# Preparing the queries for dK in a fused attention backward: one copy per 16 units, a 64 KB transpose, and a fourfold repeat through DRAM into a ring of two

## The chip, the cores and the metric

The kernel runs on one core of one Trainium2 chip. A core has a matrix engine (PE, with its weight loads listed apart as PEld), a vector engine (DVE), a scalar engine (ACT), a general engine (POOL, GpSimd) and SP, which issues DMAs; 16 DMA engines move the data. On-chip memory has 128 partitions (SBUF); PE writes to PSUM, eight banks of 128 x 512 floats. The metric is device microseconds of one execution, the median of several runs; lower is better.

## What is computed

The program is the forward output and all gradients of two attention layers side by side, on a sequence of 2048 tokens with width 448 and 16 heads of 28. Layer A is linear attention, layer B is softmax attention with a single key head and value head shared by the 16 query heads. Nearly all of the time goes into layer B:

```python
def _B_ref(x, wq, wk, wv, wo):
    q = (x @ wq).reshape(B, S, H, Dh).transpose(0, 2, 1, 3)
    k = x @ wk
    v = x @ wv
    scores = jnp.einsum("bhqd,bkd->bhqk", q, k) * (Dh ** -0.5)
    p = softmax(scores, axis=-1)
    o = jnp.einsum("bhqk,bkd->bhqd", p, v)
    return o.transpose(0, 2, 1, 3).reshape(B, S, H * Dh) @ wo
out  = concatenate([A(x_A, ...), B(x_B, ...)], axis=-1)
grads = vjp(out)(grad_out)      # for all eight inputs
```

For the backward pass of B the kernel needs, for every head, P (the exponentials), dP = dO V', dS = P * (dP - D), and from dS both dQ = dS K and dK = dS' Q, summed over all heads.

## The kernel before

Layer A and the projections of B come first (up to about 207 us of the span). Then one loop does the softmax attention of B, forward and backward fused. It is written out by hand under a manual schedule: the order of the code is the order of each engine's queue.

The loop counts units u. Two heads and 256 queries make a block b; there are 64 blocks (8 chunks qc of 256 queries, in each 8 pairs of heads), and each block has 8 units of 256 keys, so 512 units, and 28 more for the pipeline to run out. Pairs of heads lie two and two in a group g of four heads, so a group and a chunk make 16 units. What one unit issues:

- PE: the scores S of unit u and the products dP of unit w = u - 16 (rows_SD, L683), the sums for O and dQ (o_dq, L894, on even u), dV (dv_mm, L901, from u = 8b + 20), and dK (dk_m, L865, on odd u from u = 8b + 27).
- ACT: two exponentials into eT (L955, L997), and cp, a copy of half of dP out of PSUM (L971).
- DVE: the first half of dsT = dP * eT (L967), and a 32 x 32 block transpose of dsT into dsx (L1041), which dk_m reads.
- POOL: the second half of dsT (L972), and once per 8 units the small products prod, don, R (L821, L830, L831) and Dq, don (L836, L837, in row_D).
- SP: every fourth unit a DMA transpose of eT into eN, 1 MB (L999), which dv_mm reads. After five of the blocks, two or four token tiles of finished output are transposed as well (oTq, L1048).
- Spread over the units, the output projection of finished rows; a finished tile of 112 KB is stored by a DMA that POOL issues (L749).

dK needs the queries as weights in the order of dsx: in each of the four blocks of 32 partitions the same 32 queries, with the two of each pair of neighbours in separate tiles (s = 0, 1). That is qX. Until now it was made per chunk and group: qc_copy (L854) copies the 256 queries of a chunk and repeats them fourfold along the free dimension, one parity s at a time, into the staging tile qst; qc_T (L859) has SP transpose qst (256 KB) into a quarter of qX[qc]. There are two qX tiles of 256 KB x 4, one in use and one being filled, in the pools cqXa and cqXb. For chunk 0 this is done before the loop, half of the copies on DVE and half on POOL; for the next seven chunks at units 29, 30, 37, 38, 45, 46, 53 and 54 of each 64, all on POOL (the lines with gq and iq, L973 to L979 and L1001).

At u = 8b + 27 (L986) the finished dQ of block b is written over its queries, so these must have been read before.

Queues matter here in two places. POOL's instructions run in order, and a DMA that POOL issues stands among them: a wait of such a DMA holds up the dsT products behind it. SP's DMAs are issued in order as well, and a transpose is issued for as long as SP takes to describe it.

Of the kernel before, what the change touches and what calls it, by code (L numbers as in the profile page):

```python
# [11 lines left out]
BF16 = mybir.dt.bfloat16  # L12
# [5 lines left out]
P = 128  # L18
# [7 lines left out]
def kernel(  # L26
# [21 lines left out]
    nc = tc.nc  # L48
# [13 lines left out]
    dpool = ctx.enter_context(tc.tile_pool(name="dscr", bufs=1, space=bass.MemoryType.DRAM))  # L62
# [585 lines left out]
    NU = NB * 8  # L648
    qT_B = [R1[:, g, :] for g in range(4)]
    vaug, kn, do_nat = vaug_, kn_, R2x[:, 0:NS, :]  # L650
    with ExitStack() as cs_:
        pe_ = cs_.enter_context(tc.tile_pool(name="ceT", bufs=1, side="right"))
        pn_ = cs_.enter_context(tc.tile_pool(name="ceN", bufs=1, side="right"))
        pd_ = cs_.enter_context(tc.tile_pool(name="cdsT", bufs=5, side="right"))
        pqa_ = cs_.enter_context(tc.tile_pool(name="cqXa", bufs=1, side="right"))
        px_ = cs_.enter_context(tc.tile_pool(name="cdsx", bufs=2, side="right"))
        pqb_ = cs_.enter_context(tc.tile_pool(name="cqXb", bufs=1, side="right"))
        pc_ = cs_.enter_context(tc.tile_pool(name="ccp", bufs=3, side="right"))
        pw_ = cs_.enter_context(tc.tile_pool(name="cwk", bufs=4, side="right"))
        pp_ = cs_.enter_context(tc.tile_pool(name="cout", bufs=2, side="right"))  # L660
# [4 lines left out]
        dsT, dsx, qX, don, doT, rl, prod = ({} for _ in range(7))  # L665
# [3 lines left out]
        def eT(u):  # L669
            return ETs[u // 4 % 5][:, u % 4, :, :]  # L670
# [4 lines left out]
        def mmt(out, lhsT, rhs, pos, start, stop):  # L675
            nc.tensor.matmul(out, lhsT=lhsT, rhs=rhs, start=start, stop=stop, tile_position=pos,  # L676
                             skip_group_check=True)

        def blk(b):
            qc, pair = divmod(b, 8)  # L680
            return qc, pair, pair // 2, pair % 2
# [24 lines left out]

        woTp, gbT = R4, R2.rearrange("p t (c k) -> p t c k", k=P)

        qst = pp_.tile([P, 8, 4, 32], BF16, name="qst", bufs=1)[:, :, :, :]
        identF = pp_.tile([P, P], F32, name="identF", bufs=1)  # L710
        make_identity(nc, identF[:])
        oTs = pp_.tile([P, 256], F32, name="oTs", bufs=1)
# [89 lines left out]
        def due(u, lag):  # L802
            b, r = divmod(u - lag, 8)
            return b if r == 0 and 0 <= b < NB else None
# [28 lines left out]
        def row_D(b):  # L833
            Dq = pw_.tile([P, 2, 2, 1], F32, name="Dq")
            nc.vector.tensor_reduce(out=Dq[:, :, :, 0], in_=prod[b][:], axis=AX.X, op=ALU.add)
            nc.gpsimd.tensor_tensor(out=Dq[:], in0=Dq[:], in1=rl[b][:], op=ALU.mult)  # L836
            nc.gpsimd.tensor_tensor(out=don[b][:, :, :, 0:1], in0=Dq[:], in1=rl[b][:], op=ALU.mult)  # L837
# [13 lines left out]
            doT[b] = pw_.tile([P, 256], BF16, name="doT", bufs=2)  # L851
            nc.vector.tensor_copy(out=doT[b][r:r + 64, :], in_=tps2.pop(b)[r:r + 64, 0:256])  # L852

        def qc_copy(eng, st, qc, g, s):  # L854
            src = qT_B[g][:, qc * 256:(qc + 1) * 256].rearrange("p (b j s) -> p b j s", b=4, s=2)[:, :, :, s]
            eng.tensor_copy(out=st.rearrange("p (b s) a j -> p b s a j", s=2)[:, :, s, :, :],  # L856
                            in_=src.unsqueeze(2).to_broadcast([P, 4, 4, 32]))

        def qc_T(st, qc, g):  # L859
            nc.sync.dma_start_transpose(qX[qc].rearrange("p b s c -> p (b s) c")[:, :, g * P:(g + 1) * P],  # L860
                                        st.rearrange("p n a j -> p (n a j)"))

        dk_two = SB[2]

        def dk_m(b, m, other=0):  # L865
            qc, pair, g, hp = blk(b)
            h, B, s = m // 8, (m // 2) % 4, m % 2
            for a in range(4):
                rhs = dsx[b][32 * a:32 * a + 32, :, h, :, :].rearrange(
                    "p u t (b i s) -> p u t b i s", b=4, s=2)[:, :, :, B, :, s]  # L870
                k = 32 * ((a + 2) % 4) if other else 32 * a
                mmt((dk_two if other else dk_acc)[k:k + 32, :],
                    qX[qc][32 * a:32 * a + 32, B, s, pair * 64 + 32 * h:pair * 64 + 32 * h + 32],
                    rhs, (32 * a, k), other == 2 or b == 0 and m == 0, other == 0 and b == NB - 1 and m == 15)

        def o_mm(v):
# [44 lines left out]
        do_slots.update({32 + 8 * n: (13 + n // 4, n % 4 * P, n % 4 * P + P) for n in range(12)})  # L921
        with tc.manual_schedule():
            nc.sync.dma_start(wo, wo_d[:, 0:D].rearrange("(g p) c -> p g c", p=P))
            qX[0] = pqa_.tile([P, 4, 2, 512], BF16, name="qX")
            for g in range(4):
                st = pd_.tile([P, 2, 512], BF16, name="dsT").rearrange("p a (n j) -> p a n j", j=32).rearrange(
                    "p a (n b) j -> p (a n) b j", b=4)
                qc_copy(nc.gpsimd, st, 0, g, 0)
                qc_copy(nc.vector, st, 0, g, 1)
                qc_T(st, 0, g)  # L930
            for u in range(NU + 28):
                w = u - 16
                hasS = u < NU
# [5 lines left out]
                if u % 2 == 0:  # L939
                    b, n = divmod(u - 20, 8)  # L940
# [22 lines left out]
                if hasD:  # L963
                    dst = pd_.tile([P, 2, 512], BF16, name="dsT")
                    dsT[w] = dst
                    ew = eT(w)
                    nc.vector.tensor_tensor(out=dst[:, 0, :], in0=dp[0][:, :], in1=ew[:, 0, :], op=ALU.mult)  # L967
                    if (b := due(u, 12)) is not None:
                        row_D(b)
                    cp = pc_.tile([P, 512], BF16, name="cp")  # L970
                    nc.scalar.activation(out=cp[:, :], in_=dp[1][:, :], func=ACT.Copy)  # L971
                    nc.gpsimd.tensor_tensor(out=dst[:, 1, :], in0=cp[:, :], in1=ew[:, 1, :], op=ALU.mult)  # L972
                gq, iq = divmod(u % 64 - 29, 8)  # L973
                qq = u // 64 + 1
                if 0 <= gq < 4 and u < 448:
                    if gq == 0 and iq == 0:
                        qX[qq] = (pqb_ if qq % 2 else pqa_).tile([P, 4, 2, 512], BF16, name="qX")
                    if iq < 2:
                        qc_copy(nc.gpsimd, qst, qq, gq, iq)  # L979
                if u == 7:  # L980
                    nc.vector.memset(oTs[64:128, :], 0.0)
                if (b := due(u, 9)) is not None:
# [1 line left out]
                if (b := due(u, 27)) is not None:  # L984
                    qc, pair, g, hp = blk(b)
# [10 lines left out]
                if hasS:  # L996
                    nc.scalar.activation(out=eT(u)[:, 1, :], in_=sp[1][:, :], func=ACT.Exp, scale=scale)  # L997
                    if u % 4 == 3:
                        nc.sync.dma_start_transpose(ENs[u // 4 % 6][:, :, :],  # L999
                                                    ETs[u // 4 % 5][:, :, :, :].rearrange("p a b c -> p (a b c)"))  # L1000
                    if 0 <= gq < 4 and iq == 1 and u < 448:  # L1001
                        qc_T(qst, qq, gq)

                if u % 2:
                    b, i = divmod(u - 27, 8)
                    if 0 <= b < NB:
                        for m in range(2 * i, 2 * i + 4):
                            dk_m(b, m, (1 + (u == 519 and m == 2 * i + 1)) * (m % 2) if 519 <= u < 537 else 0)
                else:
                    o_dq((u - 2, u - 1), (u - 20, u - 19))  # L1010
# [26 lines left out]
                if 0 <= y < NU:  # L1037
                    b, tp = divmod(y, 8)
                    if tp == 0:
                        dsx[b] = px_.tile([P, 8, 2, 2, 256], BF16, name="dsx")  # L1040
                    nc.vector.transpose(  # L1041
                        out=dsx[b][:, tp, :, :, :].rearrange("p h t c -> p (h t c)").bitcast(F32),
                        in_=dsT[y][:, :, :].rearrange("p h c -> p (h c)").bitcast(F32))
# [20 lines left out]
        for c in range(4):  # L1064
            t = dkvT[0:32, :].rearrange("p (t a i) -> p t a i", a=4, i=32)[:, :, c, :]
            src = dk_acc[32 * c:32 * c + 32, :].rearrange("p (t i) -> p t i", i=32)
# [93 lines left out]
```

## Time and profile before

| | us |
|---|---|
| median of three runs | 1041.17 |
| lowest and highest | 1037.56, 1046.53 |
| the profiled execution | 1044.09 |
| its span on the core | 1042.4 |

The loop's first exponential (L955) starts at 207.09 us, its last at 968.48 us; the tail (dK and dV out, dWq, dX) ends at 1042.4. The granted clock of PE is 1.0 throughout. In the rows of the profile the first number of a pair is busy time in us, the second the mean of one instruction in ns, and behind the bar stands the time that the engine was idle just before these instructions, with who ended it. Instructions of one engine can overlap at their ends: three ACT instructions of some 640 ns each start every 480 to 500 ns. Some other groups:

| line, engine, what | count | mean ns |
|---|---|---|
| L967 DVE, first half of dsT | 512 | 665 |
| L1041 DVE, block transpose into dsx | 512 | 697 |
| L955, L971, L997 ACT | 512 each | 636, 639, 651 |
| L427 POOL, a copy of 128 x 256 (layer A) | 4 | 399 |
| L749 POOL, issue of a store of 112 KB | 16 | 582 |
| L538 POOL, issue of a store of 224 KB | 8 | 724 |
| L94 POOL, issue of a load of 448 KB | 4 | 760 |
| L999 SP, issue of a transpose of 1 MB | 128 | 5440 (median) |
| L860 SP, issue of a transpose of 256 KB | 32 | 1264 (median) |

### The profile page before, as it was taken

To read this page: it belongs to the slowest core of one execution; us is meant where nothing else is said; L and a number is where in the kernel's file an instruction comes from. 1 tells how busy PE (TensorE), PEld (TensorE's weight loads), DVE (VectorE), ACT (ScalarE), POOL (GpSimd) and SP (SyncE) were. 2 spreads that over 40 slices of the span, in tenths; PEclk is the share of its full clock that TensorE was granted. 3 is DMA by queue.
4 is the path that set the end of the run, shared out by engine and by line. 5 is a ranking of instruction groups with operands and counts; after the bars stand their busy time and mean duration, and the time that the engine had idled before them with its cause. 6 is when DMAs were issued, how large, how long until landed. Compare 5 with 4: busy or idle time off the path is not lost.

```text
span 1042.4 us, 40109 instructions
## 1 busy us (share of the span) xinstructions
PE 1003.5 (96%) x16245; PEld 485.1 (47%) x16245; DVE 886.9 (85%) x1780; ACT 865.2 (83%) x1743; POOL 812.3 (78%) x1106
## 2 busy tenths in 40 slices
PE   9999999999999999999999999999999999999998
PEld 5555554434444444444444444444444444444444
DVE  7897500669999999999999999999999999999942
ACT  6463132599999999999999999999999999999632
POOL 8601282238998998999999989998999999889860
PEclk9999999999999999999999999999999999999999
DMA  9879999299999999999999999999999999999983
GB/s 261 157 137 191 176 229 218 38 161 201 194 187 192 187 193 194 202 187 194 201 193 195 192 187 204 198 182 202 188 197 186 195 195 195 200 188 203 228 168 90
DMA packets 689058, 195.15 MB, mean 187 GB/s; under 512 B 670408, under 2 KB 686688, under 8 KB 688872
## 3 DMA queue, kind: packets, MB, share of 16 engines
q1 hardware_dynamic: 680392, 179.97, 105.0%
q0 software_dynamic: 4544, 9.46, 3.0%
q10 hardware_dynamic: 3936, 3.16, 1.0%
q8 instruction: 127, 2.08, 0.8%
q14 instruction: 59, 0.48, 0.2%
HBM read 12.60 MB, written 10.84 MB: 22 GB/s over the span
## 4 chain that ended last, share of the span: by engine, by line
PE 39%; DVE 25%; POOL 16%; ACT 8%; issue 7%; DMA 3%; DVEq 0%; SPq 0%; ACTq 0%; POOLq 0%
PE agen L81 13%; POOL dsT L972 12%; DVE dsT L967 10%; PE agen L676 9%; DVE dsx L1041 9%; PE aacc L676 8%; PE aacc L81 7%; ACT cp L971 4%; ACT eT L997 2%; DMA eN<-eT 2%; DVE doT L852 1%; DVE R L986 1%; POOL qst L856 1%; POOL prod L821 1%; PE aacc L809 1%
## 5 line engine op out<-in xcount | busy, mean ns | idle before, releaser
L972 POOL TENSOR_TENSOR dsT<-cp,eT 128x512 bf16<-128x512 bf16 x512 | 584.6, 1156 | 49.4 <-ACT cp L971 42.6
L1041 DVE STREAM_TRANSPOSE dsx<-dsT 128x512 f32<-128x512 f32 x512 | 356.7, 697 | 5.8 <-POOL dsT L972 3.2
L676 PEld LDWEIGHTS <-R 32*128 32x128 bf16 (+1 forms) x9104 | 245.1, 94 | 243.3 <-issue 192.5
L967 DVE TENSOR_TENSOR dsT<-agen,eT 128x512 bf16<-128x512 f32 x512 | 340.3, 665 | 11.3 <-PE agen L676 5.4
L971 ACT ACTIVATE cp<-agen 128x512 bf16<-128x512 f32 x512 | 327.0, 639 | 11.8 <-PE agen L676 9.7
L955 ACT ACTIVATE eT<-aacc 128x512 bf16<-128x512 f32 x512 | 325.5, 636 | 12.0 <-PE agen L676 6.8
L997 ACT ACTIVATE eT<-aacc 128x512 bf16<-128x512 f32 x512 | 333.4, 651 | 0.0
L676 PE MATMUL agen<-dsx,qX 32*32 32x512 bf16 x4024 | 264.0, 376 | 0.0
L676 PE MATMUL agen<-doT,R 32*128 32x256 bf16 x2048 | 243.5, 269 | 4.1 <-DVE dsT L967 3.2
L676 PE MATMUL aacc<-R,R 32*128 32x256 bf16 (+1 forms) x2240 | 207.9, 267 | 16.7 <-DVE doT L852 6.6
L676 PE MATMUL agen<-dsT,R 128*32 128x256 bf16 x2048 | 155.5, 273 | 0.5 <-issue 0.5
L676 PE MATMUL agen<-eT,R 128*32 128x256 bf16 x2048 | 155.5, 273 | 0.1
L676 PEld LDWEIGHTS <-qX 32*32 32x32 bf16 x4096 | 78.3, 89 | 112.5 <-issue 54.1
L676 PE MATMUL aacc<-eN,don 128*32 128x512 bf16 x1024 | 91.7, 387 | 1.0 <-DMA eN<-eT 1.0
L81 PEld LDWEIGHTS <-R 128*128 128x128 bf16 x517 | 40.9, 98 | 41.0 <-issue 10.6
L81 PE MATMUL agen<-R,R 128*128 128x448 bf16 (+1 forms) x180 | 42.1, 361 | 0.3 <-DVE pq L244 0.3
L676 PEld LDWEIGHTS <-don 128*32 128x32 bf16 x1024 | 21.1, 93 | 42.5 <-issue 42.5
L856 POOL COPY qst<-R 128x512 bf16<-128x512 bf16 x56 | 34.2, 611 | 5.0 <-DVE dsx L1041 2.5
L821 POOL TENSOR_TENSOR prod<-R,oTs 128x128 f32<-128x128 bf16 x64 | 27.5, 430 | 9.0 <-DVE oTs L817 9.0
L586 DVE TENSOR_TENSOR osb<-R 32x512 bf16<-32x512 bf16 x4 | 1.7, 413 | 35.4 <-DMA R<-xa 33.8
L427 POOL COPY pk<-R 128x256 bf16<-128x256 bf16 x4 | 1.6, 399 | 37.7 <-DVE R L389 37.7
L262 POOL TENSOR_SCALAR wdq<-wdq 128x448 bf16<-128x448 bf16 x16 | 21.1, 1326 | 12.0 <-DVE phiT L243 12.0
(235 smaller groups left out, 1000.1 us busy)
## 6 DMA issues: line engine op xcount, KB each, us to landing
eN<-eT SPq DMA_TRANSPOSE x128
xa<-in_A_x_dram SPq DMA_DIRECT2D x8, 224.0 KB
ga<-in_grad_out_dram SPq DMA_DIRECT2D x4, 448.0 KB
out_dram<-osb ACTq DMA_DIRECT2D x16, 112.0 KB
xa<-in_grad_out_dram POOLq DMA_DIRECT2D x4, 448.0 KB, 7.1
out_dram<-wdq POOLq DMA_DIRECT2D x8, 224.0 KB, 5.5
eT<-in_grad_out_dram SPq DMA_DIRECT2D x4, 448.0 KB
eT<-in_B_x_dram SPq DMA_DIRECT2D x4, 448.0 KB
```

Source lines behind the costliest of these rows:

```text
L81: nc.tensor.matmul(out_ap, lhsT=lhsT, rhs=rhs, start=start, stop=stop, tile_position=(0, 0))
L262: nc.gpsimd.tensor_scalar(out=wq_n[:, st, 0:D], in0=wq_n[:, st, 0:D], scalar1=1.0, scalar2=None, op0=ALU.min)
L676: nc.tensor.matmul(out, lhsT=lhsT, rhs=rhs, start=start, stop=stop, tile_position=pos, skip_group_check=True)
L809: nc.tensor.transpose(onp[:, qb, :, :].rearrange("p h c -> p (h c)"), oTs[0:64, qb * P:(qb + 1) * P], identF[0:64, 0:64], tile_position=(0 ...
L821: nc.gpsimd.tensor_tensor(out=prod[b][:], in0=dnv, in1=os_, op=ALU.mult)
L856: eng.tensor_copy(out=st.rearrange("p (b s) a j -> p b s a j", s=2)[:, :, s, :, :], in_=src.unsqueeze(2).to_broadcast([P, 4, 4, 32]))
L955: nc.scalar.activation(out=eT(u)[:, 0, :], in_=sp[0][:, :], func=ACT.Exp, scale=scale)
L967: nc.vector.tensor_tensor(out=dst[:, 0, :], in0=dp[0][:, :], in1=ew[:, 0, :], op=ALU.mult)
L971: nc.scalar.activation(out=cp[:, :], in_=dp[1][:, :], func=ACT.Copy)
L972: nc.gpsimd.tensor_tensor(out=dst[:, 1, :], in0=cp[:, :], in1=ew[:, 1, :], op=ALU.mult)
L997: nc.scalar.activation(out=eT(u)[:, 1, :], in_=sp[1][:, :], func=ACT.Exp, scale=scale)
L1041: nc.vector.transpose(out=dsx[b][:, tp, :, :, :].rearrange("p h t c -> p (h t c)").bitcast(F32), in_=dsT[y][:, :, :].rearrange("p h c -> p ...
```

## The change

The queries of one chunk and group (16 units) are copied once, without repeating them, in the order (s, j, b), both parities in one instruction: q_split, on POOL, at u = 16G + 5 for group G. SP transposes this as 64 KB into qtr. At u = 16G + 14 POOL issues a DMA that writes qtr four times into a buffer in DRAM (q_out), one buffer for each of the 32 groups. At u = 16G + 20 POOL issues a DMA that reads the buffer back as 256 KB into a tile of a ring of two (q_in), with the repeat now along the partitions. The first dk_m of the group is at u = 16G + 27. The copies and transposes before the loop, the repeated copies in it and the two large tiles are gone. The sum row_D of block 0, which stood under a condition that is not met at u = 12, is now done.

```diff
-        pqa_ = cs_.enter_context(tc.tile_pool(name="cqXa", bufs=1, side="right"))
+        pq_ = cs_.enter_context(tc.tile_pool(name="cqX", bufs=2, side="right"))
         px_ = cs_.enter_context(tc.tile_pool(name="cdsx", bufs=2, side="right"))
-        pqb_ = cs_.enter_context(tc.tile_pool(name="cqXb", bufs=1, side="right"))
...
-        qst = pp_.tile([P, 8, 4, 32], BF16, name="qst", bufs=1)[:, :, :, :]
+        qst = pp_.tile([P, 2, 32, 4], BF16, name="qst", bufs=1)[:, :, :, :]
+        qtr = pp_.tile([P, 2, P], BF16, name="qtr", bufs=1)[:, :, :]
+        q_d = [dpool.tile([512, 256], BF16, name=f"q_d{i}") for i in range(32)]
...
-        def qc_copy(eng, st, qc, g, s):
-            src = qT_B[g][:, qc * 256:(qc + 1) * 256].rearrange("p (b j s) -> p b j s", b=4, s=2)[:, :, :, s]
-            eng.tensor_copy(out=st.rearrange("p (b s) a j -> p b s a j", s=2)[:, :, s, :, :],
-                            in_=src.unsqueeze(2).to_broadcast([P, 4, 4, 32]))
-
-        def qc_T(st, qc, g):
-            nc.sync.dma_start_transpose(qX[qc].rearrange("p b s c -> p (b s) c")[:, :, g * P:(g + 1) * P],
-                                        st.rearrange("p n a j -> p (n a j)"))
+        def q_split(G):
+            qc, g = divmod(G, 4)
+            src = qT_B[g][:, qc * 256:(qc + 1) * 256].rearrange("p (b j s) -> p s j b", b=4, s=2)
+            nc.gpsimd.tensor_copy(out=qst, in_=src)
+            nc.sync.dma_start_transpose(qtr, qst.rearrange("p s j b -> p (s j b)"))
+
+        def q_out(G):
+            nc.gpsimd.dma_start(q_d[G].rearrange("(a p) c -> p a c", a=4),
+                                qtr.rearrange("p s c -> p (s c)").unsqueeze(1).to_broadcast([P, 4, 256]))
+
+        def q_in(G):
+            qX[G] = pq_.tile([P, 4, 2, P], BF16, name="qX")
+            nc.gpsimd.dma_start(qX[G].rearrange("p b s c -> p (b s c)"), q_d[G].rearrange("(p b) c -> p (b c)", b=4))
...
-                    qX[qc][32 * a:32 * a + 32, B, s, pair * 64 + 32 * h:pair * 64 + 32 * h + 32],
+                    qX[b // 2][32 * a:32 * a + 32, B, s, hp * 64 + 32 * h:hp * 64 + 32 * h + 32],
...
-            qX[0] = pqa_.tile([P, 4, 2, 512], BF16, name="qX")
-            for g in range(4):
-                st = pd_.tile([P, 2, 512], BF16, name="dsT").rearrange("p a (n j) -> p a n j", j=32).rearrange(
-                    "p a (n b) j -> p (a n) b j", b=4)
-                qc_copy(nc.gpsimd, st, 0, g, 0)
-                qc_copy(nc.vector, st, 0, g, 1)
-                qc_T(st, 0, g)
...
-                    if (b := due(u, 12)) is not None:
+                    if u > 12 and (b := due(u, 12)) is not None:
                         row_D(b)
...
-                gq, iq = divmod(u % 64 - 29, 8)
-                qq = u // 64 + 1
-                if 0 <= gq < 4 and u < 448:
-                    if gq == 0 and iq == 0:
-                        qX[qq] = (pqb_ if qq % 2 else pqa_).tile([P, 4, 2, 512], BF16, name="qX")
-                    if iq < 2:
-                        qc_copy(nc.gpsimd, qst, qq, gq, iq)
+                if u == 12:
+                    row_D(0)
+                if hasS and u % 16 == 5:
+                    q_split(u // 16)
+                if hasS and u % 16 == 14:
+                    q_out(u // 16)
+                if 0 <= u - 20 < NU and u % 16 == 4:
+                    q_in(u // 16 - 1)
...
-                    if 0 <= gq < 4 and iq == 1 and u < 448:
-                        qc_T(qst, qq, gq)
```

## The prediction

> **What bounds the kernel now.** First the page: who is busy. Then the waits inside the pass loop, where the change lies (270 to 970 us of the span).
>
> ```profile
> PE 1003.5 (96%) x16245; PEld 485.1 (47%) x16245; DVE 886.9 (85%) x1780; ACT 865.2 (83%) x1743; POOL 812.3 (78%) x1106
> ```
> ```profile
> POOL dsT L972 <- ACT cp L971: 30.5, 98, 0.6
> ...
> ACT eT L955 <- PE agen L676: 5.3, 16, 1.0
> ...
> DVE dsx L1041 <- POOL dsT L972: 3.2, 6, 1.0
> ...
> POOL qst L856 <- DVE dsx L1041: 2.5, 2, 1.3
> POOL qst L856 <- DMA qX<-qst: 2.5, 4, 1.1
> ...
> PE aacc L676 <- DMA eN<-eT: 1.0, 2, 0.8
> ```
> A row is: who, for whom, us in total, times, longest. Over 700 us ACT waits some 6 us, and the wait on the transposed queries is 2.5 us. From the starts of the exponential L955 in the timeline, 16 units take 23.56 us, again and again, and in that time ACT has no idle stretch. The excess over 23.56 sits in a few groups of 16 units: 1.73 (units 176-191), 1.06 and 0.96 (288-319), 1.30 (432-447), all while query copies run on POOL; 1.08 (400-415), where PE waits for eN; 1.61 in four others. Two neighbouring stretches by engine, one disturbed, one clean:
>
> ```profile
> 465.11:490.40 25.29, 23.46 (x464) 11.02 (x464) 23.85 (x47) 24.02 (x50) 23.65 (x31) 1.00 1.22 194
> 490.40:513.96 23.56, 23.03 (x464) 10.97 (x464) 23.20 (x47) 23.56 (x50) 21.98 (x29) 1.00 1.16 206
> ```
> Columns: length, then PE, PEld, DVE, ACT, POOL. Same work but for two copies; POOL 23.65 of 25.29 in the first, ACT 23.56 of 23.56 in the second. The chain of waits over the disturbed stretch begins:
>
> ```profile
> by line: POOL dsT L972 48.9%; issue 13.9%; DVE dsx L1041 8.4%; PE agen L676 4.0%; POOL R L831 3.2%; POOL prod L821 3.1%; POOL don L830 2.9%; POOL qst L856 2.8%; ACT cp L971 2.4%; DVE dsT L967 2.4%; PE aacc L676 2.4%; ACT eT L955 2.0%; ACT e
> ```
> So ACT sets the pace, with PE and DVE a few per cent behind, and POOL takes over when it falls behind: in the timeline L972 starts 0.1 to 1.0 us after its cp in clean stretches, up to 2.8 us in the disturbed ones; up to 1.5 us late (units 224-255) costs ACT nothing. Now SP:
>
> ```profile
> 454.25 5.89 SPq L999 DMA_TRANSPOSE eN<-eT  x1
> 460.19 1.30 SPq L860 DMA_TRANSPOSE qX<-qst  x1
> 461.60 11.66 SPq L999 DMA_TRANSPOSE eN<-eT  x2
> 473.35 1.26 SPq L860 DMA_TRANSPOSE qX<-qst  x1
> 474.72 10.65 SPq L999 DMA_TRANSPOSE eN<-eT  x2
> ```
> Start, duration. SP is never free: one eN transpose takes 5.44 us to issue and is wanted every 5.89; it starts 4 to 10.8 us after its last exponential.
>
> **The change, part by part.** SP loses 32 issues of 256 KB (1.26 to 2.0 us, 42 us with gaps) and gets 32 of 64 KB. No row has that size: a quarter of 1.26 is 0.32, the small plain issues on SP (L1019) take 0.48; I take 0.45, 32 x 0.55 with gaps = 18 us. SP gains some 25 us of air. Who waited for SP: PE 1.0 us and POOL 2.5 us, no more. The backlog drains, and eN, wanted 12 units after it is issued, hides that entirely.
>
> POOL loses 56 copies of 611 ns (34 us; L856 below) and four before the loop; DVE loses four before the loop, beside an ACT that runs from 207.09 us on unhindered: nothing. POOL gets per 16 units one copy of a quarter of the elements, one store, one load.
>
> ```profile
> L972 POOL TENSOR_TENSOR dsT<-cp,eT 128x512 bf16<-128x512 bf16 x469 | 535.4, 1156 | 34.2 <-ACT cp L971 30.5
> L856 POOL COPY qst<-R 128x512 bf16<-128x512 bf16 x52 | 31.8, 611 | 5.0 <-DVE dsx L1041 2.5 <-DMA qX<-qst 2.5
> L821 POOL TENSOR_TENSOR prod<-R,oTs 128x128 f32<-128x128 bf16 x58 | 24.9, 430 | 0.0
> L830 POOL TENSOR_TENSOR don<-R,rl 128x128 bf16<-128x128 bf16 x59 | 23.6, 400 | 0.0
> ```
> POOL's budget of 16 units: 16 x 1.156 + 2 x (0.430 + 0.400 + 0.399 + 0.202 + 0.216, L821 to L837) = 21.79 of 23.56, so 1.77 free (the timeline shows three gaps of 0.31 in 8 units, 1.88). The copy q_split has 256 elements a partition: L427 of that size takes 399 ns, but it reads a contiguous row and q_split steps 128 bytes between elements, so 0.40 to 0.75 (the slowest L856 copies average 752); nearest by size, 0.40. The store q_out has 512 rows of 512 B: L94 with 512 rows 760 ns, L538 with 256 rows 724, L749 with 128 rows 583; I take 0.76, up to 1.0. The load q_in has 128 rows: 0.58, as L749. Each issue leaves 0.07 more before the next instruction. Sum 0.40 + 0.76 + 0.58 + 0.14 = 1.88, against a mean of 56 x 0.611 / 32 = 1.07 before. That just fills the budget. The out-projection's store (0.65 every 32 units, from unit 168) did fit before and no longer does: 2 x 1.88 + 0.65 = 4.41 against 3.54 to 3.76, over by 0.65 to 0.87, some 11 times: +7 to +10 us, less one credit of about 1.5 us of lateness. I take +7. With the upper prices (0.75, 1.0) it is over by 0.6 a group more: 32 x 0.6 = +19 besides.
>
> The Trainium skill (GPSIMD Engine Reference, Performance pitfalls for Q7 kernels) states that reads with a step over 8 bytes cost half as much again per element; by that rule q_split, stepping 128 bytes, would be an estimated 0.5 us, a gain for the slower side; no row here shows such a step.
>
> In exchange the disturbed groups go: 1.73 + 1.06 + 0.96 + 1.30 + 1.08 = 6.1 us. That work of POOL comes in two clumps (0.98 us at units 4-5, 0.83 at 14), each after L972 has caught up, so lateness peaks near 1.4 us, under the 1.5 that cost nothing.
>
> The new waits. q_out waits on POOL for the small transpose; it is issued behind eN's 5.4 us from unit 3, ends near unit 10, and POOL asks at the end of unit 14: 6 us spare. q_in waits on POOL for q_out's landing, 9.0 us after L972 of unit 14; behind it queue the dsT products and all that follows from them. And PE's first dk matmul of a group (unit 27) waits for q_in: in the trace 7.0 us (6.6 to 7.7) lie between the end of L972 of unit 20 and that weight load; PE's queue of score matmuls stands behind it, then ACT. POOL's stores in the loop (112 KB, a bit under half of q_in) land so:
>
> ```profile
> DMA to landing us min/median/max: 2.1/5.4/8.3
> ```
> and the DMA engines look like this between 500 and 512 us, in 40 slices of 0.3 us:
>
> ```profile
> GB/s 291 289 288 292 291 289 288 292 291 272 251 168 9 207 202 82 3 9 10 166 289 289 291 291 289 289 291 291 287 221 251 209 155 207 104 26 12 13 279 290
> ```
> The store issued at 504.46 just missed the pause at 505; its first packet ran at 508.99, when the burst of SP's queue was over, and it landed after 7.0 us. All 14 stores landed 5.6 to 9.6 us after the start of the eN issue before them, in the next pause. Without backlog q_in is issued 3.1 us after an eN issue (that one starts 0.9 us before cp of unit 20 ends, L972 ends 2.2 us after it). A burst lasts until 0.5 us into the next eN issue, so q_in is served from 5.9 + 0.5 = 6.4 on and lands, by the stores and 0.5 us for its size, 4.8 to 7.3 us after its own issue; with 1 or 2 us of backlog (after the oTq transposes at units 130, 258, 386) a us or two later. Against 7.0 that is a wait of 0 to 0.1 us in some 20 groups and 0.3 to 1.4 in ten: +6, between 0 and the next rival but one. A late PE gives POOL time to catch up, so it overlaps with POOL's +7; together +10.
>
> The Trainium skill (DMA: Bandwidth & Descriptors, Queues, rings and completion order) says that a DMA engine takes turns between queues at packet granularity; then q_in would not wait for a burst's end; the late first packet of 504.46 speaks against it.
>
> row_D for block 0, which the old code skips (63 of 64), is done: 0.7 us in the empty start, nothing.
>
> **Sum**, against the profiled execution: 1044.1 - 6.1 + 10 = 1048, 0.4% up; on the median of 1041.2 that is 1045.
>
> **The rivals.** (a) q_in is interleaved and lands like the quickest two (2.3 and 4.4 us), so PE never waits, and POOL's overflow lives on its credit: -6 to +1, 1035 to 1042. For: those two landings; against: the other twelve. (b) POOL becomes the pace: strided copy 0.75, store 1.0: -6 + 7 + 19 = +20, 1061, or 1054 where a few groups still fit. It decides from 1.77 us of new work in 16 units; for it: the sum is at 1.88 already. (c) Slower, by PE's wait for q_in: 256 KB don't fit into one pause and the rest waits for the next, one eN period (5.9 us) later: landing at 10.7 to 13.2, PE waits 3.7 to 6.2 us. It decides where landing passes 7.0. One group in five: 6 x 5 = +30, 1065; every group: over +115, 1155 or more. Against: at 58 KB in 0.25 us (the store at 950 us) 262 KB take 1.1 us, and the pauses are 0.8 and 1.0 long with a small burst between. (d) SP's freedom is worth more than its waits show, also in the uneven units 16-31 (2.5 us over) and at the tail (0.95 us of backlog): 1028 to 1031.
>
> **How the numbers follow.** The three runs before spread from 1037.6 to 1046.5, so 1%, 10.4 us, is about what counts as a change. Forecast 0.50, (a) 0.12, (b) 0.16, (c) 0.16, (d) 0.06. Faster by over 1%: (d) and a sliver of (a), 0.07. Slower by over 1% (over 1051.6): (b), (c) and the upper end of the forecast, 0.37. Same: 0.56. The range leaves out (d) and the larger half of (c): 1033 to 1071; the likeliest case's own range is 1038 to 1053.
>
> **What would show it.** Right: L856 and its waits gone; SP idle between eN issues; POOL's idle time before L972 down from 34 us to near nothing; a wait of PE (dk weights, L675 there) for the DMA qX<-q_d, under 1.5 us at most. (b) shows as ACT cp and eT waiting on PE while POOL has no gap; (c) as 31 waits of 4 us. The forecast is wrong if q_out's landing holds POOL, or if the copy or the store is off by more than 0.3 us.

## The result and the profile after

| | before | after |
|---|---|---|
| median of four runs, us | 1040.63 | 1111.07 |
| lowest and highest | 1037.56, 1046.53 | 1099.46, 1114.56 |
| the profiled execution | 1044.09 | 1113.84 |
| its span | 1042.4 | 1112.1 |
| from the first to the last exponential of the loop | 761.4 | 823.0 |
| tail behind it | 73.9 | 81.3 |
| mean granted clock of PE | 1.000 | 0.977 |

The ratio is 1.065, with a 95% interval of 1.0555 to 1.0745. The forecast was 1045, in a range of 1033 to 1071. Of the 69.7 us that the span grew, 61.6 lie in the loop and 7.4 in the tail. First the page of the changed kernel: who is busy.

```profile
PE 1029.4 (93%) x16245; PEld 487.1 (44%) x16245; DVE 892.1 (80%) x1777; ACT 870.1 (78%) x1743; POOL 840.7 (76%) x1144
```

DVE and ACT have the same work as before within 6 us, PE 26 us more for the same instructions, POOL 28 more. None of that comes near the 62 us that the loop grew. The largest waits of the changed kernel between 270 and 1040 us of the span (who, for whom, us in total, times, longest) show where the engines stand still:

```profile
ACT eT L954 <- PE agen L675: 57.2, 62, 3.1
...
POOL dsT L971 <- ACT cp L970: 44.7, 100, 2.4
...
PEld L675 <- DMA qX<-q_d: 23.0, 22, 2.4
PE aacc L675 <- DMA eN<-eT: 17.2, 17, 2.5
PE agen L675 <- DMA qX<-q_d: 17.1, 20, 2.2
```

ACT, which hardly waited before (5.3 us for PE), waits 57.2 us for PE; POOL waits 44.7 us for ACT, where it was 30.5; and PE waits for two DMAs, 40.1 us for the repeated queries and 17.2 us for eN. Read alone, this list says that q_in is issued too late. That reading is the first theory. The second comes from SP, whose queue the list doesn't show. The issues of the eN transposes (duration in ns, least, median and longest), in the kernel before and in the changed one:

```profile
L999 SPq DMA_TRANSPOSE eN<-eT x128: 4832/5440/6272, 213.8 to 971.0; - x128
```
```profile
L999 SPq DMA_TRANSPOSE eN<-eT x128: 4818/5705/9379, 212.5 to 1039.5; - x128
```

The same 128 instructions on the same bytes take 5.42 us in the mean before and 5.91 after, up to 9.4. Their sum grew from 693.6 to 756.6, by 63.0 us, and the loop grew by 61.6. Between 700 and 760 us SP's timeline of the changed kernel (start, duration, line, number of issues) has no free place:

```profile
716.54 1.19 SPq L859 DMA_TRANSPOSE qtr<-qst  x1
717.83 23.75 SPq L999 DMA_TRANSPOSE eN<-eT  x4
741.69 1.19 SPq L859 DMA_TRANSPOSE qtr<-qst  x1
742.98 17.47 SPq L999 DMA_TRANSPOSE eN<-eT  x3
```

One group of 16 units takes SP 742.98 - 717.83 = 25.15 us here, and ACT's own pace is 23.56. It also shows the second surprise: the 64 KB transpose costs SP 1.19 us, hardly less than 256 KB did (1.26). The new work on POOL, in the same window as the waits (busy time in us, mean of one in ns, and behind the bar the idle time before it):

```profile
L971 POOL TENSOR_TENSOR dsT<-cp,eT 128x512 bf16<-128x512 bf16 x474 | 542.2, 1156 | 48.7 <-ACT cp L970 44.7 <-DVE doT L853 1.1
...
L862 POOL DMA_DIRECT2D q_d<-qtr x30 | 24.0, 799 | 12.0 <-DVE dsx L1039 3.6 <-DVE dsT L966 3.2 <-DVE oTs L983 3.2
...
L858 POOL COPY qst<-R 128x256 bf16<-128x256 bf16 x29 | 18.3, 631 | 0.0
...
L867 POOL DMA_DIRECT2D qX<-q_d x29 | 16.9, 583 | 0.8 <-issue 0.8
```

Idle time before L971 has grown to 48.7 us: POOL is not what sets the pace. And how long q_in takes from issue to landing:

```profile
DMA to landing us min/median/max: 3.8/7.8/9.7
```

The tail shows SP's backlog once more. The last eN issue starts 0.95 us after its exponential before, and 7.13 in the changed kernel. Behind it in SP's queue stands a load of grad_out that the tail's first matmuls read; PE's wait for it, in the waits around the end of the loop (965 to 1000 us before, 1035 to 1060 after):

```profile
PE aacc L81 <- DMA eT<-in_grad_out_dram: 0.2, 1, 0.2
```
```profile
PE aacc L81 <- DMA eT<-in_grad_out_dram: 6.7, 1, 6.7
```

That is nearly all of the tail's 7.4 us. Back in the loop, by the trace of the kernel before q_in is issued 7.0 us ahead of the moment when PE wants it, so the median load is late by 0.8 us. Both theories can point to a row. They differ in what happens when q_in comes in time.

### The profile page after: what moved, and what is told of

It reads as the page before. It is cut to its first block, busy times and chain, and to the rows that moved or that the text cites. A ratio compares the mean times of both kernels' runs of the same rounds, so it can differ in the third digit from the quotient of the medians.

```text
span 1112.1 us, 40169 instructions
## 1 busy us (share of the span) xinstructions
PE 1029.4 (93%) x16245; PEld 487.1 (44%) x16245; DVE 892.1 (80%) x1777; ACT 870.1 (78%) x1743; POOL 840.7 (76%) x1144
## 3 DMA queue, kind: packets, MB, share of 16 engines
q0 software_dynamic: 9664, 26.24, 10.1%
q10 hardware_dynamic: 3936, 3.16, 1.0%
## 4 chain that ended last, share of the span: by engine, by line
PE 42%; DMA 27%; POOL 10%; DVE 9%; issue 6%; ACT 5%; DVEq 0%; POOLq 0%; ACTq 0%
DMA eN<-eT 18%; PE agen L675 13%; PE agen L81 13%; PE aacc L675 9%; DMA qX<-q_d 9%; POOL dsT L971 7%; PE aacc L81 5%; DVE dsT L966 4%; ACT cp L970 3%; DVE dsx L1039 2%; ACT eT L997 1%; POOL prod L822 1%; POOL R L832 1%; DVE doT L853 1%; POOL don L831 1%
## 5 line engine op out<-in xcount | busy, mean ns | idle before, releaser
L971 POOL TENSOR_TENSOR dsT<-cp,eT 128x512 bf16<-128x512 bf16 x512 | 585.7, 1156 | 67.7 <-ACT cp L970 53.9
L675 PE MATMUL agen<-dsx,qX 32*32 32x512 bf16 x4024 | 274.5, 387 | 20.3 <-DMA qX<-q_d 17.1
L675 PE MATMUL agen<-doT,R 32*128 32x256 bf16 x2048 | 253.4, 274 | 3.1 <-DVE dsT L966 2.0
L675 PE MATMUL agen<-dsT,R 128*32 128x256 bf16 x2048 | 159.5, 277 | 1.7 <-POOL dsT L971 1.6
L675 PE MATMUL agen<-eT,R 128*32 128x256 bf16 x2048 | 158.9, 277 | 0.6 <-issue 0.5
L675 PE MATMUL aacc<-eN,don 128*32 128x512 bf16 x1024 | 101.7, 399 | 17.4 <-DMA eN<-eT 17.2
L862 POOL DMA_DIRECT2D q_d<-qtr x32 | 25.6, 800 | 12.0 <-DVE dsx L1039 3.6
```

The lines of the kernel that those rows point to most:

```text
L862: nc.gpsimd.dma_start(q_d[G].rearrange("(a p) c -> p a c", a=4), qtr.rearrange("p s c -> p (s c)").unsqueeze(1).to_broadcast([P, 4, 256]))
```

## The experiments

**Latency**: the loop waits for q_in's late landing. **Stream**: SP issues transposes back to back and the DMA engines carry them back to back; each 256 KB that passes through the same engines lengthens that stream by about 1 us, and 64 of them lengthen the loop by about 64 us, whenever they land.

The first four kernels ran on one chip, beside runs of the kernel before with a median of 1043.5 us.

### e1: all steps one group earlier

```diff
-        pq_ = cs_.enter_context(tc.tile_pool(name="cqX", bufs=2, side="right"))
+        pq_ = cs_.enter_context(tc.tile_pool(name="cqX", bufs=3, side="right"))
...
+            q_split(0)
+            q_out(0)
...
-                if hasS and u % 16 == 5:
-                    q_split(u // 16)
-                if hasS and u % 16 == 14:
-                    q_out(u // 16)
-                if 0 <= u - 20 < NU and u % 16 == 4:
-                    q_in(u // 16 - 1)
+                if u % 16 == 5 and u < NU - 16:
+                    q_split(u // 16 + 1)
+                if u % 16 == 14 and u < NU - 16:
+                    q_out(u // 16 + 1)
+                if hasS and u % 16 == 4:
+                    q_in(u // 16)
```

> The changed kernel with the three steps of a group one group (16 units) earlier and a ring of three qX tiles: the load is issued 23 units before its use, with the same instructions and the same traffic. Two theories. Latency: what costs is that q_in, issued 7.0 us before PE needs it, lands after 7.8 us; then PE's waits of 40 us on qX and the half-clock stretches behind them go, and the time falls from 1111 to 1040-1055. Stream: SP is never idle from 229 us on in either kernel, the sum of its eN issues grew from 694 to 757 us, as much as the loop (761 to 823 us), because each 256 KB that POOL sends through the DMA engines lengthens the stream of transposes by about 1 us; then the waits only move from qX to eN, SP's eN issues still sum to about 750, and the time stays above 1090.

Measured: 1109.34 us (1098.86 to 1111.92), ratio to the kernel before 1.0612 (1.0558 to 1.0667). No wait for qX is left. Some waits of this kernel, 270 to 1040 us:

```profile
ACT eT L956 <- PE agen L675: 44.3, 46, 3.1
...
PE aacc L675 <- DMA eN<-eT: 23.9, 25, 2.3
...
POOL q_d L862 <- DMA qtr<-qst: 5.7, 3, 3.2
```

The largest wait for a DMA in the changed kernel, 40 us, was taken away, and the time stayed (1111.07 before this edit, with a spread of 15 us). PE now waits for eN instead, 23.9 us against 17.2. Latency falls as the cause: the time does not hang on q_in's late landing.

### e2: the traffic alone, added to the kernel before

```diff
+        q_d = [dpool.tile([512, 256], BF16, name=f"q_d{i}") for i in range(64)]
...
+        def q_out(G):
+            nc.gpsimd.dma_start(q_d[G].rearrange("(a p) c -> p a c", a=4),
+                                R3f[:, 4096:4352].unsqueeze(1).to_broadcast([P, 4, 256]))
...
+                if hasS and u % 16 == 14:
+                    q_out(u // 16)
+                if 0 <= u - 20 < NU and u % 16 == 4:
+                    q_out(32 + u // 16 - 1)
```

> The kernel before, whole, with two stores of 256 KB per 16 units added (units 14 and 4 of each 16, on POOL, of constant data into DRAM buffers that nothing reads): the change's traffic and POOL issues without its waits. Latency: nobody waits for these, so only POOL's added 1.7 us per 16 units counts, on top of its copies: 1045-1065. Stream: 64 x 1 us more in SP's stream, eN issues summing to about 750 us, PE waiting on eN, 1090-1115.

Measured: 1109.8 us (1107.17 to 1114.84), ratio 1.0627 (1.0594 to 1.066). Nothing reads these stores, and the queries are prepared as of old. The queue lines (packets, MB, the time of the packets as a share of 16 engines' span), of the kernel before and of this one:

```profile
q1 hardware_dynamic: 680392, 179.97, 105.0%
q0 software_dynamic: 4544, 9.46, 3.0%
```
```profile
q1 hardware_dynamic: 680392, 179.97, 98.7%
q0 software_dynamic: 9664, 26.24, 8.8%
```

q0, POOL's queue, carries 26.24 MB, to the byte what it carries in the changed kernel; before it was 9.46, and 64 x 256 KB lie between. Its packets took 98.0 us (8.8% of 1113.1) against 31.3 before (3.0% of 1042.4), 66.7 us more or 1.04 us for each 256 KB. The packets of SP's queue, q1, took no longer: 1098.6 against 1094.5 (e5 below, with the same packets, has 1081). A share above 100% says that packets overlap. The eN issues sum to 762.6 us, 69.0 more than before: 1.08 us for each 256 KB. The loop takes 823.9.

So the whole loss of the change is had with none of its steps but the transfers and their issues on POOL. Could it be POOL, which now has stores on top of its copies? Its waits, and PE's, in this kernel between 270 and 1040 us:

```profile
POOL dsT L977 <- ACT cp L976: 35.4, 72, 2.4
PE aacc L676 <- DMA eN<-eT: 23.9, 19, 3.2
POOL qst L857 <- DMA qX<-qst: 17.8, 15, 2.2
```

POOL waits for ACT at least as long as before (30.5), and 17.8 us for the old qX transposes, which are late with the rest of SP's queue; it does not set the pace. e7 and e9 below vary the bytes and the issuing engine.

### e3 and e4: one of the two transfers

e3 keeps the first group's store and lets all loads read its buffer; e4 keeps the stores, and loads only for the first two groups, whose tiles are used again.

```diff
# e3
+            nc.gpsimd.dma_start(qX[G].rearrange("p b s c -> p (b s c)"), q_d[0].rearrange("(p b) c -> p (b c)", b=4))
...
+                    q_out(u // 16) if u < 16 else None
# e4, in q_in
+            if G > 1:
+                qX[G] = qX[G % 2]
+                return
```

> The changed kernel with only the first group's store: all loads read that one buffer, so the output of dK is of the wrong queries; the loads, their place and PE's wait for them are as in the change. Latency: q_in lands as late as before (7.5-8 us against 7.0), so most of the loss stays: 1085-1110. Stream: half of the added traffic is gone, eN issues sum to about 725 us, half of the loss goes: 1065-1085.

> The changed kernel with loads for the first two groups only: the later groups use these two tiles again, so dK is of the wrong queries; all stores stay. Latency: no load, no wait: 1035-1050. Stream: half of the added traffic stays and nothing holds PE back on qX, so PE waits on eN instead: 1065-1085, eN issues summing to about 725 us.

Measured, one run each: 1072.79 with the loads, 1080.12 with the stores. Against 1043.5 that is 29 and 37 us, so each half costs about half; 7 us between two single runs are less than the spread of the changed kernel. The stores lie under no wait of PE, and cost about as much as the loads, which do: what counts is the traffic, not who waits for it.

The next four kernels ran beside runs of the kernel before with a median of 1043.24.

### e5: the old copies, spread over the group

```diff
-                gq, iq = divmod(u % 64 - 29, 8)
-                qq = u // 64 + 1
-                if 0 <= gq < 4 and u < 448:
+                qq, gi = divmod(u - 29 + 64, 64)
+                gq, iq = gi // 16, gi // 8 % 2
+                hasQ = gi % 8 == 0 and 29 <= u < 477
+                if hasQ:
...
```

One repeated copy every 8 units, where the kernel before has two of four groups in a row; no bytes are added.

> The kernel before with its query copies spread: one per 8 units (at units 29, 37, ... 85 of each chunk's 64) instead of two in neighbouring units of every second half; transposes and traffic as before. POOL then has 0.61 us in each 8 units against 0.9 free and is never late. Stream: SP's 1.26 us transposes are spread evenly as well, so its backlog keeps lower peaks, but its sum stays; the disturbed groups (some 6 us) go: 1034-1040 against 1043. If the pace of the kernel before is set by SP's sum alone, no change: within 2 us.

Measured: 1042.34 us (1040.26 to 1043.44), ratio 0.9987 (0.9976 to 0.9998). SP's timeline of this kernel (as above) is even, one qX transpose to four of eN:

```profile
696.43 21.72 SPq L999 DMA_TRANSPOSE eN<-eT  x4
718.20 1.30 SPq L860 DMA_TRANSPOSE qX<-qst  x1
719.60 22.11 SPq L999 DMA_TRANSPOSE eN<-eT  x4
741.76 1.34 SPq L860 DMA_TRANSPOSE qX<-qst  x1
743.21 21.53 SPq L999 DMA_TRANSPOSE eN<-eT  x4
```

The disturbed groups are mostly gone (between 270 and 970 us ACT's L955 waits for PE's L676 1.2 us, before 5.3). But 743.21 - 719.60 = 23.61 us of SP stand against ACT's 23.56, and the sum of SP's issues is 732.7, before 736.5. An even order gains next to nothing, about a tenth of a per cent. The first expectation was 2 to 8 us too low; the second, that a pace set by SP's sum would not change by more than 2 us, is what came.

### e6: the kernel before without the later query copies

Copies and transposes for chunks 0 and 1 alone; their tiles serve the other six chunks.

```diff
-                        qX[qq] = (pqb_ if qq % 2 else pqa_).tile([P, 4, 2, 512], BF16, name="qX")
-                    if iq < 2:
+                        qX[qq] = qX[qq % 2] if qq > 1 else pqb_.tile([P, 4, 2, 512], BF16, name="qX")
+                    if iq < 2 and qq < 2:
...
-                    if 0 <= gq < 4 and iq == 1 and u < 448:
+                    if 0 <= gq < 4 and iq == 1 and qq < 2:
```

> The kernel before without the copies and transposes of chunks 2 to 7 (their dK uses the queries of chunks 0 and 1): 24 issues of 1.36 us taken from SP, 48 copies from POOL. Stream: eN issues still sum to 690-700 us, SP gets idle for the first time, some 25 us; ACT is then the only bound, 1030-1037. Latency makes no statement but that of POOL's copies: the same.

Measured, one run: 1036.97, loop 754.4. After the first two, most groups of 16 units take 23.56 us and none more than 24.16, and for the first time SP is idle: 49.4 us. This is ACT's floor: whatever is done for the queries, this loop can gain some 0.6%. The eN issues here:

```profile
L999 SPq DMA_TRANSPOSE eN<-eT x128: 4777/5324/5863, 214.3 to 963.5; - x128
```

They sum to 671.6 us, 22.0 less than before, where 690 to 700 was expected, and SP is idle twice as long as the 25 us of the expectation. So each of the 24 query transposes that are gone was worth some 0.9 us of eN's issues besides its own 1.36. Whether they held the eN issues up, or an issue is shorter when SP was idle before it, no run separates.

### e7: e2 with 64 KB stores

```diff
-            nc.gpsimd.dma_start(q_d[G].rearrange("(a p) c -> p a c", a=4),
-                                R3f[:, 4096:4352].unsqueeze(1).to_broadcast([P, 4, 256]))
+            nc.gpsimd.dma_start(q_d[G][0:P, :], R3f[:, 4096:4352])
```

> As the kernel before with two stores per 16 units, but of 64 KB instead of 256 KB (the tile stored once, not four times). If the stream is lengthened by the bytes: 64 x 0.25 us more in eN's issues, about 710 us, 1050-1062 us. If each intrusion costs, whatever its size: about 750 us, 1090-1110.

Measured, one run: 1059.53. As many transfers as in e2 and a quarter of the bytes give eN issues of 709.7 us, 16.1 more than before: 0.25 us for each 64 KB. POOL issues as many DMAs as in e2, at 0.58 us each where those took 0.79, so the issues are not what costs: the price goes by bytes.

### e8: the changed kernel without its traffic

Stores and loads for the first two groups only; the 64 KB transposes and the copies stay.

```diff
+            if G > 1:
+                qX[G] = qX[G % 2]
+                return
...
+                    q_out(u // 16) if u < 32 else None
```

> The changed kernel with stores and loads for the first two groups only; the copies and the 64 KB transposes stay (later groups use the first two tiles, so dK is of the wrong queries). Stream: with no traffic eN's issues sum to 690-700 us and the time is that of the kernel before or a little less, 1033-1045; with 0, 32, 32 and 64 transfers of 256 KB the times then stand as 1038, 1073, 1080 and 1110. If it stays above 1060, the 64 KB transposes themselves disturb the stream.

Measured, one run: 1048.3, a little above what was expected. The loop takes 761.1, as before the change, and SP's idle time is 1.0 us: the small transposes fill SP's queue as the large ones did. In the profiled executions the 4 us over the kernel before lie in the tail (77.7 against 73.9): the last eN issue starts 5.2 us after its exponential.

### e9: e2's stores from ACT's queue

```diff
-            nc.gpsimd.dma_start(q_d[G].rearrange("(a p) c -> p a c", a=4),
+            nc.scalar.dma_start(q_d[G].rearrange("(a p) c -> p a c", a=4),
```

> The kernel before with the same two stores of 256 KB per 16 units of constant data as in the run that added this traffic on POOL's queue, but issued by ACT's queue; nothing reads them. If the transposes are lengthened because the bytes pass through the same DMA engines, the issues of eN sum to 750 to 765 us as there (5.42 us each before, 5.9 here), and the time is about 1100 to 1115. If they are lengthened because POOL makes its descriptors in software, the sum stays near 694 and the time at 1041 to 1055 (64 issues on ACT, the engine that sets the pace before, may cost some 0.1 to 0.2 us each, 6 to 13 us).

Measured, one run: 1091.03, beside 1045.54 for the kernel before. It lies between the two expectations, and so do the eN issues, which sum to 731.6 us. An issue takes ACT 0.366 us, 23.4 us for 64, so ACT's floor alone would be some 754 + 23 = 777; the loop takes 803.7. The sum of all of SP's issues for eN and the queries is 46.5 us over that of the kernel before, 0.73 us for each 256 KB, where the same bytes from POOL cost 1.07. So most of the price is paid whoever issues the transfers, and POOL is not needed for it. About a third hangs on how they are sent, and the runs differ in two ways there: in the queue, and in the packets. ACT's queue (q10, which had 3936 packets and 3.16 MB before) takes 33792 packets for these bytes, where q0 took 5120 in e2:

```profile
q10 hardware_dynamic: 37728, 19.94, 7.5%
```

Which of the two counts is not settled, and e9 is one run.

### The runs together

Loop, from the first to the last exponential; the sums of SP's issues for eN and for the queries; "rest" is the loop less both. All in us; the time is the median of the runs (one run for e3, e4 and e6 to e9), the others are from the profiled execution.

| kernel | time | loop | eN | queries | rest |
|---|---|---|---|---|---|
| before | 1040.63 | 761.4 | 693.6 | 42.9 | 24.9 |
| after | 1111.07 | 823.0 | 756.6 | 40.6 | 25.8 |
| e1, steps earlier | 1109.34 | 808.6 | 741.4 | 42.8 | 24.4 |
| e2, traffic added to before | 1109.8 | 823.9 | 762.6 | 42.1 | 19.2 |
| e3, loads only | 1072.79 | 782.8 | 714.8 | 41.1 | 26.9 |
| e4, stores only | 1080.12 | 788.4 | 726.8 | 41.6 | 20.0 |
| e5, before with copies spread | 1042.34 | 757.7 | 689.0 | 43.7 | 25.0 |
| e6, before with few copies | 1036.97 | 754.4 | 671.6 | 10.2 | 72.6 |
| e7, 64 KB stores added to before | 1059.53 | 775.8 | 709.7 | 42.8 | 23.3 |
| e8, after without traffic | 1048.3 | 761.1 | 694.2 | 41.3 | 25.6 |
| e9, e2's stores from ACT | 1091.03 | 803.7 | 731.6 | 51.4 | 20.7 |

In ten of eleven kernels the rest is 19 to 27 us: the gaps of some 0.1 us between issues, the transposes of oTq, and the ends. The loop is as long as SP's stream. A queue that always has a backlog fills its loop whatever sets the pace, so this alone proves nothing; what does is that the stream and the loop grow with the bytes that are added (e7, e3, e4, e2), and are back where they were without them (e8). Only in e6, where SP has 49.4 us to spare, ACT sets the time. (The profiled execution of e1 is its fastest of four, that of the changed kernel is among its slowest, so the 14 us between their loops are not a gain of e1; the medians are 2 us apart.)

The Trainium skill (DMA: Bandwidth & Descriptors, Issuing engines are not separate DMA queues) says that DMAs of the scalar, sync and gpsimd engines all run on the same 16 DMA engines and interleave, whoever started them. e2 agrees, with 1.08 us of transposes lost for each 256 KB that POOL sends, and so does e9, with 0.73 for ACT.

## Why the prediction was wrong

**What bounds the kernel.** "So ACT sets the pace" was half of it. The pace of ACT was read rightly: 23.56 us, e6's in most groups. But SP was just as full. By the prediction's own rows four eN issues of 5.44, one of 1.26 and five gaps of some 0.1 are 23.5 us of those 23.56. And I had the row: "SP is never free". I valued it by who waited for it, 1.0 and 2.5 us, and not by its load. Those waits were small because the queue just fitted. And the 5.44 us for a transpose, taken as the time that SP needs to describe it, is no fixed cost of the instruction: the mean was 5.42 us in the kernel before, 5.91 with the change's traffic and 5.25 in e6. How the engines' load comes back to the issue no run shows.

**"eN, wanted 12 units after it is issued, hides that entirely"** is the step that failed. It was said of a backlog that would drain; it grew. From 270 us on, the eN issue starts 6.9 us (median) after its last exponential in the kernel before, 8.5 and up to 13.3 in the changed one, and 0.03 in e6. Twelve units of distance hide a late transpose; they don't hide a queue that needs more time per group than the group has. With 1.19 for the small transpose and two transfers at 0.98 each (63.0 / 64) the group of 23.5 us becomes 25.4; the loop measured 823.0 / 32 = 25.7.

**The term that is missing** from the sum is the traffic. The prediction has the price: rival (c) works out that 262 KB take 1.1 us, and uses it to see whether a load fits into one pause. 64 such transfers are 70 us; added to a queue with nothing free they would have given a loop of 761 + 70 = 831, measured 823. The pauses in the rate of the DMA engines looked like free room; e2, whose stores nobody waits for, shows that a transfer costs the transposes its 1.08 us all the same.

**SP's relief**, 25 us, did not come. "A quarter of 1.26 is 0.32 ... I take 0.45": measured 1.19, and the sum of the query issues fell from 42.9 to 40.6 (the prediction's "42 us with gaps" is this sum without gaps). The scaling by size had no row behind it. e8 shows what it was worth: with that transpose and no traffic SP is as full as before. So rival (d), SP's freedom, could not occur.

**POOL's budget** was nearly right. The store measured 0.80 (taken 0.76), the load 0.583 (0.58), the strided copy 0.631 (0.40, between 0.40 and 0.75). The last was too near the contiguous row. The Trainium skill (GPSIMD Engine Reference, Performance pitfalls for Q7 kernels) has half as much again per element for long steps; on the contiguous 0.399 that would be an estimated 0.60, so the rule agrees with 0.631 and the prediction's 0.5 from it was too low. POOL was over budget as forecast, but rival (b) did not come, since its work for 16 units, 23.9 us with the measured prices, now has 823.0 / 32 = 25.7: its idle time before L971 rose instead of falling.

**q_out's wait** for the small transpose, "6 us spare", was too much: the issue of the small transpose ended 1.4 to 5.7 us before q_out, and POOL waited in eight of the 32 groups, about 3 us each in three of them, behind oTq transposes, and up to 1.3 in the others. That is 12 us in all, a follow-on of SP's backlog.

**q_in's wait** had the right mechanism and the wrong size. Landing was forecast at 4.8 to 7.3 us and measured at 3.8 to 9.7 with a median of 7.8; PE waited 40 us in all, not 6. But e1 shows that this is not where the time went, and so rival (c), 1065 for one group in five and over 1155 for every group, named the right sign by a mechanism that does not decide.

**The disturbed groups** (-6.1): e6, which is 6.3 us under its kernel before, has the gain that was forecast, but there SP is free as well. In e5 POOL's copies no longer crowd and SP is as full as ever, and the median gains 1 us. So POOL's copies, to which the prediction put the 6.1 us, are not shown to be worth them. **row_D of block 0** cost nothing visible, as said.

**The signs.** None of the prediction's signs of being wrong came: POOL sat idle 0.8 us in all before the loads, so q_out's landing did not hold it; the copy was off by 0.23 us and the store by 0.04. The loss came by a way that it did not watch. Two of its signs of being right failed, though: SP was not idle between eN issues, and POOL's idle time rose.

**The clock** was not foreseen; it is below.

## What to carry to other kernels

A queue without idle time has no room, even when the list of waits hardly names it; ask for every change how much it adds to that queue per period, against the period. Data that goes through DRAM is not free because it lands in time: its bytes, at a rate that the trace shows, are added to the stream of the DMA engines that others need. And the issue of a smaller transfer is not cheaper in proportion unless a row of that size says so.

## What was unexpected of the hardware

The issue of a DMA transpose takes SP 1.19 us for 64 KB, 1.26 for 256 KB and 5.4 for 1 MB: between 64 and 256 KB the size hardly counts here.

PE's clock was halved after short pauses. In the changed kernel 13 stretches at half clock, 52 us in all, stand in the trace. Eleven of them, 44 us, lie in the loop, each 3.41 or 6.83 us long, and each begins 1.1 to 4.0 us after the start of a PE pause of 1.1 to 2.5 us. Not every such pause is followed by one: behind 1.68 us at 371.6 there is none. One of them in the windows view (from:to, length, then busy time and instructions of PE, PEld, DVE, ACT and POOL, granted clock, DMA share, GB/s):

```profile
345.60:347.43 1.83, 0.00 (x1) 0.00 (x0) 0.83 (x2) 0.55 (x2) 1.75 (x4) 1.00 1.30 80
347.43:348.50 1.07, 1.07 (x17) 0.36 (x20) 0.30 (x1) 0.35 (x1) 0.32 (x1) 0.99 1.28 287
348.50:351.92 3.42, 3.42 (x47) 1.08 (x39) 2.51 (x5) 2.80 (x6) 2.09 (x4) 0.50 0.96 214
```

PE stands still for 1.83 us, works for 1.07 at full clock, and then runs 3.42 us at half. The Trainium skill (TensorE: Matmul & The Clock Gate, Part 1: The HAM clock gate) gives half rate after at least one idle window of about 3.4 us; the length agrees with these 3.41 us, but here half clock followed a pause of half that length, with work between. Half of the 51 us that lie within the span is PE's 26 us more of busy time. What it adds to the loop by itself was not isolated. It can't be more than half of the loop's 44 us, 22 of 61.6. And in e7 the loop grew by 14.4 us with a single such stretch of 3.41 us, where the kernel before has none in its loop: most of the loss is there without it.
